# A transformer block on one core: residual sums moved from VectorE to accumulating DMAs, PSUM copies to ScalarE, b2 by DMA, and four more seven-product row pairs

## The chip, the cores and the metric

The kernel runs on one core of a Trainium2 chip. The time is device microseconds of one execution, input and output in HBM, all stages included. Three runs of the kernel before took 364.31, 365.56 and 367.79 us; the median, 365.56, is what the time after is compared with.

## What is computed

One block over 2048 rows of width 576: a layer norm, sliding dilated attention (32 heads of 18, eight keys at distances 0, 2, ..., 14), an output projection with a residual, two layer norms in a row, an MLP of width 4608 with tanh GELU, and a second residual.

```
qkv = (layernorm(x) @ wqkv)                       # 576 -> 3 x 576
logits = q . k[s - 2w] * 18**-0.5, w = 0..7       # masked where s - 2w < 0
o = softmax(logits) . v[s - 2w]
h = x + o @ wo
y = layernorm(layernorm(h))
out = h + (gelu(y @ w1 + b1) @ w2 + b2)           # 576 -> 4608 -> 576
```

## The kernel before

Row s = 16 p + j of the input lies in partition p of tile j, so a tile is 128 rows and there are 16. Keys at even distances are then other tiles of the same parity, with a shift by one partition where the tile number wraps. `kv_ring[r]` holds K and V of the eight tiles of parity r; after tile j has used its own slot, `halo(j, t)` (L336) reloads that slot from `kv_dram` one row shifted, for the tiles that come later in `ATT_ORDER`. In `pv_sum(c)`, `pv_sum(d)` the V halo of tile c must therefore land before the first product of tile d.

The first 68 us compute layer norm and QKV. Then come eight groups of two tiles, `GROUPS`, k = 0 to 7, each of about 36 us. In a group, MLP1 (`mlp1`, 4 visits of two "duos" of PSUM banks) makes the hidden values of the group's two tiles, and MLP2 (`mlp2` in groups 0 and 1, `mlp2_fast` in groups 2 to 7) makes their outputs. Everything else of later tiles is laid into this by hand: the whole schedule is written out, so each engine's queue runs in the order in which the Python emits, with waits on what is not ready. TensorE, ScalarE, VectorE, SP (plain DMAs and DMA transposes) and GpSimd have one queue each. The attention of the tiles two groups on, the projection by wo (`wo_visit`) and layer norm 2 of the next group's tiles c and d lie inside group k.

MLP1 and wo use half-height matmuls in two phases: `phase` 1 of a duo swaps the halves of its banks, and waits for `marker`, a GpSimd no-op which waits for the last matmul of phase 0 (L226). GpSimd's queue thus stands in TensorE's path.

`mlp2_fast` (L682) multiplies row pairs m = 0 to 17 of w2. For the first `rows` of them it uses a scheme of seven products in place of eight, and `plain` does the rest. `ROWS` gives 12, 12, 12, 16, 18 and 18 for groups 2 to 7. The seven products need sums of blocks: `w2_sums` of the weights (once, kept), `h_sums` of the hidden values (each group), both on VectorE. Its list `steps` is the order of work; products are tuples, "b", "d" and "f" are seed copies on ScalarE from one PSUM bank to another (L735), and names like "hc", "h", "6", "7", "in", "exp", "4" are hooks into which the main loop puts work of other tiles. For groups 3 to 6 it begins: wo visit, "hc" (h of tile c and its statistics on ScalarE), product 1, seed "b", "h", product 7, product 2, product 6.

The residual: `x_of(j)` is one of the eight even slots of `x_all`, used by tile j and by its neighbour j + 1 in turn. It holds x until `ln2_h` (L455) forms h = x + wo output. Then it is given h + b2 in one of two ways: `add_b2` on VectorE (groups 0 and 7), or `put_b2`, a DMA of b2 from SBUF, followed by `accumulate_h`, an accumulating DMA of h issued by GpSimd (groups 1 to 6). At the end of MLP2 VectorE adds the PSUM result to it and writes `o_sb`, which SP stores to the output: `finish_out` (L741) in groups 0 and 1; in `mlp2_fast`, `out0` for tile j0 (step "o0"), `do_rest` and `out1` for tile j1 (steps "rest" and "o1"). `reload_x` later loads the x of the other tile into the slot.

Of the kernel before, what the change touches and what calls it, by code (L numbers as in the profile page):

```python
# [17 lines left out]
def kernel(  # L18
# [12 lines left out]
    nc = tc.nc  # L31
# [46 lines left out]
    b2_bc = wpool.tile([P, D], BF16, name="b2_bc")  # L78
# [419 lines left out]
    def add_b2(j):  # L498
        nc.vector.tensor_tensor(out=x_of(j), in0=h_of.pop(j)[:], in1=b2_bc[:], op=ALU.add)

    def put_b2(j):
        nc.sync.dma_start(out=x_of(j), in_=b2_bc[:])

    def accumulate_h(j):
        ins = nc.gpsimd.dma_start(out=x_of(j), in_=h_of.pop(j)[:], accum_op=ALU.add).ins
        tc.add_manual_dep(ins, read[0].name, sync_dep, reason="behind the transposes of LN2")
# [108 lines left out]
    def s_slot(t, m0, m1):  # L615
# [5 lines left out]
        if not ring1_free[0]:  # L621
            return q_all[:, 11 - 2 * i, (m0 - SR) * P:(m1 - SR) * P].bitcast(F16).rearrange("p (m c) -> p m c", c=P)
# [59 lines left out]
    def mlp2_fast(g, rows, tags, wo, hooks, first_wo=False):  # L682
        last = wo is None
# [5 lines left out]
        o0, o1 = (late.tile([P, D], BF16, tag="o_sb", name="o_sb", bufs=2) for _ in range(2))  # L689
        flat = kv_ring[int(rows == NM)][:].rearrange("p w t d -> p (w t d)")  # L690
        rest = q_all[:, 13:16:2, :].bitcast(F32) if SR < rows < NM else halves(flat[:, W * 2 * D - 2 * D:W * 2 * D].bitcast(F32))
# [5 lines left out]
        def out0(n0, n1):  # L697
            add(halves(o0[:])[:, n0:n1], af[:, n0:n1, 0:HALF], halves(x_of(j0))[:, n0:n1])
            nc.sync.dma_start(out=out3[:, j0, n0 * HALF:n1 * HALF], in_=o0[:, n0 * HALF:n1 * HALF])

        def out1():
            add(o1[:, 0:HALF], b, rest[:, 0])
            add(o1[:, HALF:D], bank[5], rest[:, 1])
            nc.sync.dma_start(out=out3[:, j1, :], in_=o1[:])

        def do_rest():
            add(rest, bank[7].unsqueeze(1).to_broadcast([P, 2, HALF]), halves(x_of(j1)))
# [17 lines left out]
        elif not last:  # L725
            steps = ["wo", "hc", (1, all_), "b", "h", "e", (7, lo), (6, all_), "6", "d", "7", (2, all_), (7, hi), "rest", "in",
                     (5, all_), "f", (4, all_), "o1", (3, all_), "o0"]
# [11 lines left out]
    po_of = {}  # L739

    def finish_out(j):  # L741
        o_sb = late.tile([P, D], BF16, tag="o_sb", name="o_sb", bufs=2)
        nc.vector.tensor_tensor(out=o_sb[:].rearrange("p (g c) -> p g c", g=2), in0=po_of.pop(j)[:, :, 0:HALF],
                                in1=halves(x_of(j)), op=ALU.add)
        nc.sync.dma_start(out=out3[:, j, :], in_=o_sb[:])
# [5 lines left out]
    with tc.manual_schedule(engines={ENG.PE, ENG.Activation, ENG.DVE, ENG.SP, ENG.Pool}):  # L751
# [21 lines left out]
        nc.sync.dma_start(out=b2_bc[:], in_=B_b2.partition_broadcast(P))  # L773
# [98 lines left out]
        def ln2_ins(c, d):  # L872
            for j in (c, d):
                ln2_in(j)
            if c not in (GROUPS[2][0], GROUPS[-1][0]):
                accumulate_hs(c, d)
# [13 lines left out]
        for n, v in enumerate((19, 20, 21, 22)):  # L890
# [19 lines left out]
            18: [c_(ln2_rstd, A[0]), c_(add_b2, A[0]), c_(ln2_bias, A[0]), c_(halo, A[2], 1), c_(att_qk_add, A[2], ((0, 0, 9),))],  # L910
            19: [c_(ln2, A[1])],
            20: [c_(ln2_rstd, A[1]), c_(add_b2, A[1]), c_(ln2_bias, A[1]), c_(att_qk_rest, A[2], 0, 1)],
# [63 lines left out]
        ROWS = {2: 12, 3: 12, 4: 12, 5: 16, 6: NM, 7: NM}  # L976
# [3 lines left out]
        for k, g in enumerate(GROUPS):  # L980
# [3 lines left out]
            if k in (1, 2):  # L984
                m1[0].append(c_(finish_out, GROUPS[k - 1][1]))
            if k == 0:
                m1[0] += [c_(halos, 1), c_(load_w2, 4), c_(att_qk_a, d), c_(att_qk_rest, d, 1), c_(halo, d, 1)]
                mid[0] = {1: [c_(exps, d)]}
                m1[1] = [c_(pv_t, c), c_(pv_t, d), c_(att_qk_a, e), c_(halo, e, 1)]
# [4 lines left out]
                ib[0] = [c_(finish_out, g[0]), c_(att_den, e, f), c_(pv_sum, e), c_(send_o, e)]  # L994
                ib[8] = [c_(read_o, e)]
            elif k == 1:
                m1[0] += [c_(pv_sum, d), c_(send_o, d)]
                m1[1] = [c_(att_qk_a, e), c_(halo, e, 1), c_(read_o, d), c_(att_qk_b, e, 0), c_(halos, 7)]
                m1[3] = [c_(att_qk_a, f), c_(halo, f, 1), c_(att_qk_add, f, ((0, 0, 9), (0, 0, 4)))]
# [3 lines left out]
                ib[0] = [c_(finish_out, g[0])]  # L1003
# [88 lines left out]
```

## Time and profile before

| what | value |
|---|---|
| runs | 364.31, 365.56, 367.79 us |
| profiled execution | 364.48 us, span 362.70 |
| TensorE busy, matmuls | 357.4 us (99%), 4891 |
| VectorE busy | 302.0 us (83%) |
| ScalarE busy | 229.5 us (63%) |
| GpSimd busy | 36.7 us (10%) |
| DMA, hardware queue q1 | 41.13 MB, 41.8% of 16 engines |
| DMA, software queue q0 (GpSimd's) | 1.77 MB, 4.7% of 16 engines |
| start of MLP1, groups 0 to 7 | 68.67, 106.73, 144.48, 180.98, 217.25, 253.53, 289.62, 325.67 us |

Busy time is the union of an engine's instructions; those that only issue a DMA or wait are not counted, but the accumulating DMAs on GpSimd are shown with the time that their issue takes. Lines of an engine in order of time give start (us from the start of the span), duration (of all the instructions merged in the line), engine, source line, operation, output and inputs, shapes, count, and in brackets the idle time before it and what ended it. A "border" below is the time at which MLP1 of a group starts.

### The profile page before, as it was taken

What the parts mean: (1) busy time and instruction counts of PE and PEld (TensorE: products, weight loads), DVE (VectorE), ACT (ScalarE), POOL (GpSimd) and SP (SyncE); (2) the same over time, 40 slices, a digit from 0 to 9 for tenths busy, and PEclk for the clock granted to TensorE, in tenths of its full rate; (3) what the DMA queues carried; (4) which work ended last, traced back from release to release, by engine and by line L of the source; (5) the groups of instructions that cost most, each with busy time, mean ns of one, the idle gap of its engine ahead of it and who ended that gap; (6) DMA issues with size and microseconds to landing.
All of it is one profiled execution on the core that took longest, in us unless ns stands there. A gap on an engine that the chain in (4) does not pass through costs nothing.

```text
span 362.7 us, 11409 instructions
## 1 busy us (share of the span) xinstructions
PE 357.4 (99%) x4891; PEld 290.0 (80%) x4891; DVE 302.0 (83%) x422; ACT 229.5 (63%) x507; POOL 36.7 (10%) x47
## 2 busy tenths in 40 slices
PE   8999999999999999999999999999999999999996
PEld 5688777888788877887788778877887788778874
DVE  5899999999999998999899989998899999720431
ACT  4789756798626782668556945694569466706620
POOL 2241004000120020101100210020101100100000
PEclk9999999999999999999999999999999999999999
DMA  8995969973446732621443154514542442120001
GB/s 241 308 264 143 292 175 287 386 254 72 150 88 106 215 122 66 129 63 51 121 88 89 52 126 80 90 51 95 111 78 64 56 93 65 39 54 18 2 2 33
DMA packets 61139, 43.70 MB, mean 120 GB/s; under 512 B 31888, under 2 KB 59408, under 8 KB 61088
## 3 DMA queue, kind: packets, MB, share of 16 engines
q1 hardware_dynamic: 59200, 41.13, 41.8%
q0 software_dynamic: 1728, 1.77, 4.7%
q8 instruction: 38, 0.62, 0.7%
q10 hardware_dynamic: 160, 0.07, 0.1%
q14 instruction: 13, 0.11, 0.1%
HBM read 21.10 MB, written 12.42 MB: 92 GB/s over the span
## 4 chain that ended last, share of the span: by engine, by line
PE 93%; DMA 3%; ACT 1%; DVE 1%; issue 0%; SPq 0%; ACTq 0%
PE pm L217 38%; PE po L664 25%; PE pq L217 14%; PE po L576 10%; PE pw L217 5%; DMA oT<-td 2%; ACT h_all L557 1%; DMA xnT<-xd 1%; PE xt_pt L182 1%; DMA x_all<-in_A_x_dram 1%; DVE kv_ring L644 0%; PE xt_pt L186 0%; ACT q_all L816 0%; PE h_pt L182 0%; PE o_pt L182 0%
## 5 line engine op out<-in xcount | busy, mean ns | idle before, releaser
L557 ACT ACTIVATE h_all<-pm,b_sb 128x256 f16<-128x256 f32 (+1 forms) x288 | 108.7, 496 | 70.2 <-PE pm L217 69.6
L217 PE MATMUL pm<-hnT,w_sb 64*128 64x256 bf16 x2304 | 143.0, 269 | 0.0
L217 PEld LDWEIGHTS <-w_sb 64*128 64x128 bf16 x2304 | 111.7, 94 | 15.1 <-issue 1.7
L664 PEld LDWEIGHTS <-h_all 128*128 128x128 f16 x512 | 49.4, 98 | 14.4 <-issue 1.6
L217 PE MATMUL pq<-wq_sb,xnT 64*128 64x288 bf16 x768 | 54.4, 283 | 0.4 <-DMA xnT<-xd 0.4
L217 PEld LDWEIGHTS <-xnT 64*128 64x128 bf16 x864 | 41.4, 94 | 11.6 <-DMA xnT<-xd 0.7
L348 DVE TENSOR_TENSOR prod<-prod 128x2304 bf16<-128x2304 bf16 (+1 forms) x64 | 44.2, 691 | 2.0
L394 DVE TENSOR_TENSOR prod<-kv_ring,probs 128x4608 bf16<-128x4608 bf16 x16 | 40.9, 2555 | 2.5 <-DMA kv_ring<-kv_dram 2.1
L342 DVE TENSOR_TENSOR prod<-kv_ring,q_all 128x4608 bf16<-128x4608 bf16 x16 | 40.8, 2548 | 0.2
L217 PE MATMUL pm<-hnT,w1h_sb 64*128 64x256 bf16 x288 | 39.2, 269 | 0.0
L664 PE MATMUL po<-w2a_sb,h_all 128*128 128x288 bf16 (+1 forms) x282 | 38.9, 286 | 0.0
L400 DVE TENSOR_TENSOR prod<-prod 128x2304 bf16<-128x2304 bf16 (+1 forms) x32 | 33.9, 1058 | 1.1
L576 PEld LDWEIGHTS <-h_all 128*128 128x128 bf16 x288 | 27.9, 98 | 7.9 <-issue 1.0
L664 PEld LDWEIGHTS <-kv_ring 128*128 128x128 f16 x252 | 24.6, 98 | 6.3
L478 POOL TENSOR_TENSOR ln_rstd<-ln_var,mhalf 128x1 f32<-128x1 f32 x13 | 11.7, 899 | 169.7 <-ACT ln_var L477 169.7
L576 PE MATMUL po<-w2a_sb,h_all 128*128 128x288 bf16 x224 | 28.5, 286 | 0.0
L664 PE MATMUL po<-w2b_sb,h_all 128*128 128x288 bf16 (+1 forms) x142 | 21.5, 286 | 0.2 <-DVE h_all L644 0.2
L217 PE MATMUL pw<-wo_sb,oT 64*128 64x288 bf16 x256 | 19.6, 283 | 0.4 <-DMA oT<-td 0.3
L644 DVE TENSOR_TENSOR kv_ring<-h_all 128x1536 f16<-128x1536 f16 (+3 forms) x9 | 6.8, 753 | 15.3 <-ACT h_all L557 15.3
L735 ACT COPY po<-po 128x288 f32<-128x288 f32 x18 | 6.9, 384 | 19.3 <-PE po L664 19.3
L162 POOL TENSOR_TENSOR ln_rstd<-ln_veps,mhalf 128x1 f32<-128x1 f32 (+2 forms) x14 | 13.4, 967 | 48.5 <-DVE ln_veps L156 33.2
L217 PEld LDWEIGHTS <-oT 64*128 64x128 bf16 x288 | 13.6, 94 | 4.9 <-DMA oT<-td 1.1
(110 smaller groups left out, 387.5 us busy)
## 6 DMA issues: line engine op xcount, KB each, us to landing
w_sb<-in_B_w_dram SPq DMA_DIRECT2D x6, 768.0 KB, 6.8
kv_ring<-kv_dram SPq DMA_DIRECT2D x28, 144.0 KB, 2.8
w2a_sb<-in_B_w_dram SPq DMA_DIRECT2D x4, 1008.0 KB, 7.4
kv_dram<-kv_ring SPq DMA_DIRECT2D x13, 288.0 KB, 3.0
out_dram<-o_sb SPq DMA_DIRECT2D x15, 144.0 KB, 2.7
td<-q_all SPq DMA_DIRECT2D x14, 144.0 KB, 1.9
td<-hn SPq DMA_DIRECT2D x14, 144.0 KB, 1.8
x_all<-in_A_x_dram SPq DMA_DIRECT2D x12, 144.0 KB, 2.8
```

What stands on the lines that cost most here:

```text
L162: nc.gpsimd.tensor_tensor(out=rstd[:], in0=veps[:], in1=mhalf[:].to_broadcast([P, n]), op=ALU.pow)
L217: last = nc.tensor.matmul(duo["g"][r ^ swap][i], lhsT=lhsT, rhs=rhs, start=(swap == 0 and i == 0 and kt == 0), stop=(swap == 1 and kt == K ...
L342: nc.vector.tensor_tensor(out=prod[:], in0=k_ring[j % 2], in1=q_all[:, j, :].unsqueeze(1) .to_broadcast([P, W, D]), op=ALU.mult)
L348: nc.vector.tensor_tensor(out=prod[:, :, o * H:o * H + n], in0=prod[:, :, a * H:a * H + n], in1=prod[:, :, c * H:c * H + n], op=ALU.add)
L394: nc.vector.tensor_tensor(out=prod[:].rearrange("p w (d h) -> p w d h", h=H), in0=v_ring[j % 2].rearrange("p w (d h) -> p w d h", h=H), in ...
L400: nc.vector.tensor_tensor(out=prod[:, 0:n, :], in0=prod[:, 0:n, :], in1=prod[:, n:2 * n, :], op=ALU.add)
L478: nc.gpsimd.tensor_tensor(out=rstd[:], in0=var[:], in1=mhalf[:], op=ALU.pow)
L557: pace[0] = nc.scalar.activation(out=hT(grp)[:, f, 0:N], in_=ps[:, r, i * N:(i + 1) * N], func=ACT.Gelu_apprx_tanh, bias=b1_sb[:, f:f + 1] ...
L576: nc.tensor.matmul(banks[half], lhsT=hT(grp)[:, f, i * P:(i + 1) * P], rhs=w2_rows(f)[:, half * HALF:(half + 1) * HALF], start=(f == 0), s ...
L644: nc.vector.tensor_tensor(out=s_slot(t, m0, m1), in0=a, in1=b, op=alu)
L664: nc.tensor.matmul(bank, lhsT=l, rhs=r, start=start, stop=stop, skip_group_check=True)
L735: nc.scalar.copy(out=bank[seed[step][1]], in_=bank[seed[step][0]])
```

## The change

- In groups 0 to 5 the output is summed in `x_of(j)`: ScalarE copies the PSUM result to a float32 `o_sb`, GpSimd adds it to `x_of(j)` by an accumulating DMA (`out_sum`), and SP stores `x_of(j)` (`out_store`). For tile j1 in groups 2 to 5, ScalarE copies the common part ("rest"), and VectorE's two half adds join it to the two banks. Groups 6 and 7 keep the adds of before.
- `b2_bc` is gone; `put_b2` reads b2 from HBM, broadcast over the partitions, for all sixteen tiles, and `add_b2` is gone.
- The accumulates of h move: out of `ln2_ins` (hook "in") into hook "4", behind step "o1"; those of groups 0 and 1 into visits 1 and 2 of their own MLP1.
- Group 4 has 16 seven-product row pairs in place of 12; the w2 sums of pairs 12 to 15 that are still missing are made in group 4 (before `h_sums` ahead of MLP1's last visit) in place of group 5.

```diff
-    def add_b2(j):
-        nc.vector.tensor_tensor(out=x_of(j), in0=h_of.pop(j)[:], in1=b2_bc[:], op=ALU.add)
-
     def put_b2(j):
-        nc.sync.dma_start(out=x_of(j), in_=b2_bc[:])
+        nc.sync.dma_start(out=x_of(j), in_=B_b2.partition_broadcast(P))
...
         def out0(n0, n1):
-            add(halves(o0[:])[:, n0:n1], af[:, n0:n1, 0:HALF], halves(x_of(j0))[:, n0:n1])
+            if summed:
+                nc.scalar.copy(out=halves(o0), in_=af[:, :, 0:HALF])
+                return
+            add(halves(o0)[:, n0:n1], af[:, n0:n1, 0:HALF], halves(x_of(j0))[:, n0:n1])
...
         def out1():
+            if summed:
+                add(o1[:, HALF:D], bank[5], o1[:, 0:HALF])
+                add(o1[:, 0:HALF], b, o1[:, 0:HALF])
+                out_sum(j1)
+                return
...
         def do_rest():
+            if summed:
+                nc.scalar.copy(out=o1[:, 0:HALF], in_=bank[7])
+                return
...
+    def out_sum(j):
+        nc.gpsimd.dma_start(out=x_of(j), in_=o_of.pop(j), accum_op=ALU.add)
+
+    def out_store(j):
+        nc.sync.dma_start(out=out3[:, j, :], in_=x_of(j))
 
     def finish_out(j):
-        o_sb = late.tile([P, D], BF16, tag="o_sb", name="o_sb", bufs=2)
-        nc.vector.tensor_tensor(out=o_sb[:].rearrange("p (g c) -> p g c", g=2), in0=po_of.pop(j)[:, :, 0:HALF],
-                                in1=halves(x_of(j)), op=ALU.add)
-        nc.sync.dma_start(out=out3[:, j, :], in_=o_sb[:])
+        nc.scalar.copy(out=halves(new_o(j, True)), in_=po_of.pop(j)[:, :, 0:HALF])
...
         def ln2_ins(c, d):
             for j in (c, d):
                 ln2_in(j)
-            if c not in (GROUPS[2][0], GROUPS[-1][0]):
-                accumulate_hs(c, d)
...
-        ROWS = {2: 12, 3: 12, 4: 12, 5: 16, 6: NM, 7: NM}
+        ROWS = {2: 12, 3: 12, 4: 16, 5: 16, 6: NM, 7: NM}
...
             if k in (1, 2):
                 m1[0].append(c_(finish_out, GROUPS[k - 1][1]))
+                m1[1], m1[3] = [c_(accumulate_hs, *g)], [c_(out_store, GROUPS[k - 1][1])]
+                m1[2] = [c_(out_sum, GROUPS[k - 1][1])]
+            elif 2 < k < 7:
+                m1[0].append(c_(out_store, GROUPS[k - 1][1]))
+                m1[1], m1[3] = [c_(out_sum, GROUPS[k - 1][0])], [c_(out_store, GROUPS[k - 1][0])]
+            if k == 2:
+                m1[0].append(c_(out_store, GROUPS[1][0]))
...
-                ib[0] = [c_(finish_out, g[0]), c_(att_den, e, f), c_(pv_sum, e), c_(send_o, e)]
-                ib[8] = [c_(read_o, e)]
+                ib[0] = [c_(finish_out, g[0]), c_(out_sum, g[0]), c_(att_den, e, f), c_(pv_sum, e), c_(send_o, e)]
+                ib[8] = [c_(read_o, e), c_(out_store, g[0])]
...
+                if k == 4:
+                    m1[3] += [c_(w2_sums, 12, 14, (2, 3)), c_(w2_sums, 14, 16, (2, 3))]
                 m1[3] += [c_(h_sums, 0, min(rows, SR), early)]
...
                 x["in"] = [c_(ln2_ins, c, d)] + x["in"]
+                x["4"] = [c_(accumulate_hs, c, d)] + x["4"]
```

`m1[v]` is emitted before visit v of MLP1; `ib[f]` before row f of the second tile's MLP2.

## The prediction

> **What bounds the kernel now.** I read the page first, then stages, then each engine in order of time around the borders between groups.
>
> From the page: busy shares, granted clock and chain of waits.
>
> ```profile
> PE 357.4 (99%) x4891; PEld 290.0 (80%) x4891; DVE 302.0 (83%) x422; ACT 229.5 (63%) x507; POOL 36.7 (10%) x47
> ...
> PEclk9999999999999999999999999999999999999999
> ...
> PE 93%; DMA 3%; ACT 1%; DVE 1%; issue 0%; SPq 0%; ACTq 0%
> ```
>
> TensorE is the bound and the clock is full. Busy times by stage show whether it is also packed; the rows are groups 3, 4, 5 and 6 (start of MLP1 to the next group's start).
>
> ```profile
> 180.98:217.25 36.27, 36.27 (x495) 30.26 (x496) 33.20 (x37) 23.96 (x57) 4.99 (x6) 1.00 0.39 88
> 217.25:253.53 36.28, 36.28 (x495) 30.28 (x496) 33.31 (x37) 23.95 (x57) 2.82 (x3) 1.00 0.40 77
> 253.53:289.62 36.09, 35.99 (x490) 29.71 (x492) 33.35 (x42) 22.93 (x56) 3.80 (x6) 1.00 0.43 80
> 289.62:325.67 36.05, 35.71 (x489) 29.60 (x490) 26.22 (x38) 19.70 (x49) 2.17 (x4) 1.00 0.28 63
> ```
>
> The first two numbers after the window are its length and TensorE's busy time: groups 3 and 4 have no gap. Two remain, in the wo visits of groups 5 and 6, where TensorE waits for the transposed attention output oT. TensorE in order of time:
>
> ```profile
> 271.65 0.29 PE L217 MATMUL pw<-woh_sb,oT 64*128 64x288 bf16 x2
> 272.03 0.66 PE L217 MATMUL pw<-wo_sb,oT 64*128 64x288 bf16 x8
> ...
> 307.74 0.29 PE L217 MATMUL pw<-woh_sb,oT 64*128 64x288 bf16 x2
> 308.37 0.66 PE L217 MATMUL pw<-wo_sb,oT 64*128 64x288 bf16 x8 [0.34 <-DMA oT<-td]
> ```
>
> Elsewhere the next piece starts 0.12 us after the two-matmul piece; here 0.38 and 0.63, so 0.26 and 0.51 us are lost. So little can be won; what decides is how close to late the engines that feed TensorE are. VectorE has 33 of 36 us, and group 4 shows the margin. VectorE, ScalarE and TensorE in order of time:
>
> ```profile
> 234.60 0.88 DVE L644 TENSOR_TENSOR kv_ring<-h_all 128x1536 f16<-128x1536 f16 x1
> 235.52 0.96 DVE L644 TENSOR_TENSOR h_all<-h_all 128x1536 f16<-128x1536 f16 x1
> 236.80 1.42 DVE L458 TENSOR_TENSOR h<-pw,x_all 128x576 f32<-128x576 f32 x2 [0.33 <-PE pw L217]
> ...
> 237.64 0.77 ACT L475 ACTIVATE hn<-h 128x576 bf16<-128x576 f32 x1
> ...
> 239.63 0.39 ACT L735 COPY po<-po 128x288 f32<-128x288 f32 x1
> ...
> 237.18 4.58 PE L664 MATMUL po<-w2a_sb,h_all 128*128 128x288 bf16 x36
> ```
>
> VectorE makes h with only 0.33 us to spare; ScalarE takes the statistics of h and then the seed copy of step "b", which ends at 240.02. TensorE's product 2 adds into the bank which that copy reads, and comes 24 matmuls after 237.18: 24 x 0.1235 = 2.96, at 240.14 (0.1235 is group 3's 16.28 us of MLP2 over 132). A later h delays TensorE almost one for one.
>
> **The change part by part.** All sums are against the profiled execution: 364.48 us, of which 362.70 is span. The median of the runs is 1.08 above it, added at the end.
>
> *Products.* Group 4 goes from 12 to 16 seven-product pairs: four matmuls fewer, -4 x 0.1235 = -0.49 us on TensorE.
>
> *VectorE.* Removed: four finish_out adds and four add_b2 (0.749 each), four o0 and four rest adds of groups 2 to 5 (0.756): 12.0 us. Added: group 4's h_sums for pairs 12 to 15, 1.49 (group 5's four ran from 277.45 to 278.94). Moved: two w2_sums calls, 1.47 (278.94 to 280.41), from group 5's MLP2 to ahead of group 4's h. Most of the relief is not on TensorE's path; where it falls matters. Losing o0, VectorE starts pv_sum of the next group 0.9 us earlier in groups 3 and 4 (180.79 against 181.69; 217.07 against 217.97), since the old add waited for the last matmul.
>
> *ScalarE.* Eight 128x576 copies (0.65, the nearest row is L312 from PSUM) and four of 128x288 (0.384): 6.7 us. They hide: between the last exp table work and the first gelu of the next group ScalarE idles 5.56 us (251.17 to 256.73), and the copy of "rest" falls where it waits 1.0 for TensorE. Queued behind them are gelus; without that cover each would cost its duration. I take 0.
>
> *GpSimd.* Accumulating DMAs go from 12 to 28 (16 for h, 12 for outputs). This is what the issues, the landings and the queue show now:
>
> ```profile
> L505 POOL DMA_DIRECT2D x_all<-h x12: 886/1122/1236, 106.0 to 289.4; - x12
> DMA to landing us min/median/max: 3.1/3.9/5.5
> ...
> q0 software_dynamic: 1728, 1.77, 4.7%
> ```
>
> Behind them on GpSimd's queue stand the markers that let TensorE swap halves of a bank; the first one after a border is needed 2.2 us after MLP1 starts (two first phases of 20 matmuls, 0.055 each). At the last border into group 5 the two accumulates ended at 255.41, MLP1 having begun at 253.53: 1.88 after it. Three in a row could end 2.4 after it. Bounds 0 and 1.2 us (one more issue) at a border; at the borders into groups 3 and 4 they end 1.05 and 0.32 after it, so I take 0. The Trainium skill (SBUF, State Buffer, the section with the "DVE blocks DMA" trap) warns that a VectorE instruction in a two-port mode keeps GpSimd from writing descriptors, and elsewhere on the page that tensor_tensor has no such mode. By the warning alone each issue could wait for one 2.56 us add and three would break the margin; the rows above, 886 to 1236 ns beside a VectorE 92% busy, show no such wait.
>
> *DMA engines.* The q0 share is 0.047 x 362.7 / 12 = 1.42 us of all sixteen engines for one accumulate; sixteen more are 23 us, off the path except where somebody waits. Somebody does: in pv_sum, tile d's first product needs the halo that SP fetches after tile c's. VectorE, SP and GpSimd around the border into group 5:
>
> ```profile
> 261.16 2.56 DVE L394 TENSOR_TENSOR prod<-kv_ring,probs 128x4608 bf16<-128x4608 bf16 x1 [1.70 <-DMA kv_ring<-kv_dram]
> ...
> 256.82 0.33 SPq L339 DMA_DIRECT2D kv_ring<-kv_dram  x1
> ...
> 253.63 1.78 POOL L505 DMA_DIRECT2D x_all<-h  x2 [9.66 <-DMA x_all<-in_A_x_dram]
> ```
>
> The halo came 1.41 us after the accumulates' end and landed 4.3 us after issue, against a median of 2.8; after a gap of 2.24 (group 3) nobody waited. In the change VectorE is 0.9 earlier in groups 3 and 4, so the gap falls to about 1.35, and the output sum of j0 is issued just then (behind the second marker, 2.2 after MLP1's start). So tile d starts between 0.9 earlier (halo unhindered) and 1.6 later (halo 5.2 us after issue) than now; I take 0.7 later, as the gap matches group 5's. The Trainium skill (DMA: Bandwidth & Descriptors, Anatomy of one DMA) gives 2.0 us plus bytes over 436 GB/s for a GpSimd DMA, an estimate of 2.3 us for 147 KB. By it the accumulates would be gone when the halo comes and the sum below would be -0.9; the rows say 3.9, so the sum goes by the rows.
>
> *What that does to TensorE.*
> - Group 3: h is late by 0.7 - 0.40 (idle before it now) = 0.3, less 0.12 margin: 0.2 (0 to 1.1).
> - Group 4: 0.7 + 1.47 - 0.33 = 1.84 late; sixteen pairs put product 2 at 28 matmuls, 3.45, and the seed now ends 2.84 after MLP2's start, so 0.61 is free: 1.2 (0 to 2.1).
> - Start of group 5's MLP1: hnT follows the late h, and no gap exists now: 0.3 (0 to 1.0).
> - Group 5's oT: tile d again behind the accumulates, while MLP1 starts 0.49 earlier: 0.5 (0 to 1.1) in place of 0.26.
> - Group 6: VectorE was last there (the old rest waited for nothing at 288.40) and loses 1.47 + 0.756 ahead of it: the 0.51 gap goes (or stays).
>
> *SP.* Twelve output stores now read x_all and wait for an accumulate. At a border the first stands ahead of the halo: issued about 2.4 before MLP1's start, plus 3.9, it is released at +1.5, and SP needs to be free at +2.4. Cover 0.9 us; beyond it the halo is late, inside the 1.6 above. The second is issued after the visits' oT reads and waits for nothing. Sixteen put_b2 read HBM instead of twelve reading SBUF: 2.0 us now, 2.8 for x from HBM, needed ten us later: 0. Dropping the early load of b2 (behind all loads of x): 0.
>
> *Groups 0 to 2.* finish_out moves to ScalarE behind its exps (104.29 in group 0, where GpSimd's accumulates stood at 105.96 anyway); its results are read by nobody for 4 us or more; accumulates moved into MLP1 come one visit later, with 3.9 us between the last marker of a visit and the first need of the next. 0; bounds 0 and 0.5.
>
> Sum: -0.49 + 0.2 + 1.2 + 0.3 + (0.5 - 0.26) - 0.51 = +0.94: 365.4 profiled, 366.5 as a median. Lower ends: -0.49 - 0.26 - 0.51 = -1.26: 364.3. Upper ends: -0.49 + 1.1 + 2.1 + 1.0 + 0.84 + 0 + 0.5 = +5.0: 370.6.
>
> **The rivals.**
> *Clean gain.* Halos pass the accumulates and nothing is late: 364.3. For it: no gap at all in groups 2 to 4 now, and 10.5 us less work on VectorE. Against it: margins of 0.12 to 0.61 us and the 1.70 us wait already seen. It needs tile d's start no later than now.
> *Accumulates swamp the borders: slower.* The DMA share is 0.82 to 0.85 in the four us around a border already, with two accumulates; four stand there afterwards. If the halo has both output sums in front of it, tile d is one more accumulate (1.42) beyond the upper end in groups 3, 4 and 5: 370.6 + 4.3 = 374.9. It decides from a halo landing 0.9 us later than I take it at these three borders: +2.7 us, 369.2. Between that and the far end I price it at 371, near the upper ends.
> *The relief is worth more than 1%.* TensorE would have to lose 3.66 us of work or gaps; only 1.26 are in sight.
>
> **How the numbers follow.** About 1% (3.66 us) is what a measurement of this kernel tells from no change. The forecast, a small loss within 1%, gets 0.42; the clean gain 0.20; swamped borders 0.34; faster by over 1% 0.04. So faster 0.04, same 0.62, slower 0.34. Time 366.5; the range, 363.9 (clean gain, less what runs differ) to 371, leaves out the far end of the swamped case.
>
> **What would show it.** TensorE waits on ScalarE's seed copy in group 4's MLP2 (after 28 matmuls), on oT in group 5, and no longer in group 6; VectorE waits for kv_ring in pv_sum of groups 3 to 5. It is wrong if VectorE shows no such waits, if TensorE waits on GpSimd's markers, or if SP stands at an output store while a halo is due.

## The result and the profile after

| what | before | after |
|---|---|---|
| median of 18 runs of each (lowest to highest) | 365.57 us (364.31 to 370.23) | 369.55 us (367.46 to 371.81) |
| time after / before, 95% interval | | 1.010 (1.0073 to 1.0127) |
| profiled execution, its span | 364.48, 362.70 us | 368.69, 366.88 us |

The kernel became slower by 4.0 us, 1.0%: on the border between "no change" and "slower by over 1%". The forecast was 366.5, the range 363.9 to 371.0.

First the page of the changed kernel: busy shares, clock, the software DMA queue, the chain of waits.

```profile
PE 357.8 (98%) x4887; PEld 292.2 (80%) x4887; DVE 293.0 (80%) x410; ACT 235.6 (64%) x519; POOL 49.8 (14%) x63
...
PEclk9999999999999999999999999999999999999999
...
q0 software_dynamic: 4032, 4.13, 10.2%
...
PE 69%; DVE 14%; DMA 9%; issue 3%; ACT 2%; SPq 2%; POOL 1%; DVEq 0%; POOLq 0%; ACTq 0%
```

TensorE has its four matmuls less, the clock is as full as before, and VectorE lost 9 us (the prediction had 10.5). All of that is as intended. But the share of TensorE in the chain of waits fell from 93% to 69%, while VectorE's rose from 1 to 14 and that of DMA from 3 to 9: there are now times at which TensorE waits for VectorE, and VectorE for a DMA. GpSimd's queue takes 10.2% of the DMA engines in place of 4.7.

Busy times by stage say where. The rows are groups 0, 3, 4, 5 and 6 of the kernel after; the columns are the window, its length, and busy time of TensorE matmul, TensorE weight load, VectorE, ScalarE and GpSimd, then clock, DMA share and GB/s.

```profile
69.09:109.27 40.18, 38.41 (x509) 31.17 (x504) 35.23 (x46) 29.60 (x64) 4.25 (x5) 1.00 0.60 178
...
183.52:219.79 36.27, 36.27 (x494) 30.27 (x494) 31.75 (x36) 24.82 (x59) 5.03 (x8) 1.00 0.47 96
219.79:258.38 38.59, 36.33 (x489) 29.86 (x489) 34.79 (x44) 25.44 (x60) 6.09 (x6) 1.00 0.43 83
258.38:294.17 35.79, 35.79 (x489) 29.80 (x490) 32.78 (x39) 24.40 (x59) 4.94 (x7) 1.00 0.48 91
294.17:329.90 35.73, 35.71 (x488) 29.61 (x488) 22.66 (x32) 19.27 (x48) 3.71 (x5) 1.00 0.40 79
```

And group 0 of the kernel before, which the prediction did not show:

```profile
68.50:106.67 38.17, 38.17 (x509) 31.29 (x504) 36.69 (x47) 28.55 (x62) 2.14 (x3) 1.00 0.56 171
```

Here group 0 is counted from the first matmul of MLP1; the 68.67 and 106.73 of the table of before are where the chain of waits enters the groups, a little later. Two groups lost time: group 0 (40.18 against 38.17, +2.01) and group 4 (38.59 against 36.28, +2.31). Group 3 is as long as before, groups 5 and 6 are 0.30 and 0.32 shorter. Start-up, ahead of group 0, is 0.59 longer, which is no more than executions differ by: in the six profiled kernels with the start-up of before, group 0 begins between 68.50 and 70.33. Groups 1, 2 and 7 are 0.11 shorter together. The sum is +4.18, the difference of the spans.

**Group 4.** All engines in order of time, kernel after; "DVE L457" makes h, "ACT L743" are the seed copies "b" (243.85) and "d" (249.90), "ACT L174" at 249.13 is layer norm's second pass over tile d, "POOL L477" its reciprocal root.

```profile
239.30 0.94 DVE L641 TENSOR_TENSOR kv_ring<-h_all 128x1536 f16<-128x1536 f16 x1
239.78 1.89 PE L661 MATMUL po<-w2a_sb,h_all 128*128 128x288 bf16 x14
240.28 0.96 DVE L641 TENSOR_TENSOR h_all<-h_all 128x1536 f16<-128x1536 f16 x1
241.15 1.42 DVE L457 TENSOR_TENSOR h<-pw,x_all 128x576 f32<-128x576 f32 x2
241.94 0.69 ACT L474 ACTIVATE hn<-h 128x576 bf16<-128x576 f32 x1 [1.50 <-DVE h L457]
...
243.85 0.39 ACT L743 COPY po<-po 128x288 f32<-128x288 f32 x1
244.10 0.75 POOL L477 TENSOR_TENSOR ln_rstd<-ln_var,mhalf 128x1 f32<-128x1 f32 x1 [20.41 <-ACT ln_var L476]
...
244.29 1.88 PE L661 MATMUL po<-w2a_sb,h_all 128*128 128x288 bf16 x14 [0.70 <-ACT po L743]
...
245.81 2.55 DVE L341 TENSOR_TENSOR prod<-kv_ring,q_all 128x4608 bf16<-128x4608 bf16 x1
...
246.32 2.45 POOL L477 TENSOR_TENSOR ln_rstd<-ln_var,mhalf 128x1 f32<-128x1 f32 x1 [1.47 <-ACT ln_var L476]
...
248.80 0.30 ACT L482 ACTIVATE ln_nmean<-ln_nmean,ln_rstd 128x1 f32<-128x1 f32 x1 [1.54 <-POOL ln_rstd L477]
...
249.13 0.87 ACT L174 ACTIVATE hn<-h,ln_nmean,ln_rstd 128x576 bf16<-128x576 f32 x1
249.90 0.39 ACT L743 COPY po<-po 128x288 f32<-128x288 f32 x1
...
250.34 1.63 PE L661 MATMUL po<-x_all,kv_ring 128*128 128x288 f16 x12 [0.99 <-ACT po L743]
...
258.38 0.61 PE L216 MATMUL pm<-hnT,w_sb 64*128 64x256 bf16 x8 [0.53 <-DMA hnT<-td]
```

MLP2 starts at 239.78 and h is made 1.37 us behind it; before it was made 0.38 ahead of MLP2 (236.80 against 237.18). From there everything is late in a row: the seed copy "b" (TensorE waits, first matmul 0.87 late), GpSimd's second reciprocal root, which takes 2.45 us where the first took 0.75, the pass over tile d behind it, the seed copy "d" behind that on ScalarE's queue (TensorE 1.15 late), and hnT of the next group (0.69 late). Product 7 starts another 0.20 late: its first matmul, at 241.96, follows the first half of h, which ends at 241.91 and reads the bank that product 7 takes (in two later runs the profile names h for the wait at this place). So TensorE starts its matmuls 2.9 us late in all; four fewer matmuls (0.49) leave about the 2.3 by which the group grew.

Why the second reciprocal root takes so long can be read from the kernel before, where the same pair of instructions stands in group 4; there nothing waited for it:

```profile
241.01 2.55 DVE L342 TENSOR_TENSOR prod<-kv_ring,q_all 128x4608 bf16<-128x4608 bf16 x1
...
242.10 1.87 POOL L478 TENSOR_TENSOR ln_rstd<-ln_var,mhalf 128x1 f32<-128x1 f32 x1 [1.59 <-ACT ln_var L477]
```

In both kernels it begins while VectorE's 2.55 us product runs, and ends 0.41 us after that product has ended (243.97 after 243.56; 248.77 after 248.36).

**Group 0.** All engines in order of time, kernel after; L338 is the reload of a halo, L501 an accumulate of h, L393 VectorE's product in `pv_sum`, L192 the write of tile c's attention output to `td` in HBM, and L198 its transpose back as oT.

```profile
72.13 1.05 POOL L501 DMA_DIRECT2D x_all<-h  x1 [9.48 <-PE pm L216]
...
75.97 0.88 POOL L501 DMA_DIRECT2D x_all<-h  x1 [2.78 <-PE pm L216]
...
79.73 0.34 SPq L192 DMA_DIRECT2D td<-q_all  x1
...
83.90 2.56 DVE L393 TENSOR_TENSOR prod<-kv_ring,probs 128x4608 bf16<-128x4608 bf16 x1 [2.85 <-DMA kv_ring<-kv_dram]
...
84.47 1.22 SPq L198 DMA_TRANSPOSE oT<-td  x1
...
87.41 0.66 PE L216 MATMUL pw<-wo_sb,oT 64*128 64x288 bf16 x8 [1.34 <-DMA oT<-td]
```

And the kernel before:

```profile
81.10 2.56 DVE L394 TENSOR_TENSOR prod<-kv_ring,probs 128x4608 bf16<-128x4608 bf16 x1
...
81.75 2.31 SPq L199 DMA_TRANSPOSE oT<-td  x1
```

The halo is issued at 77.05 and `td` written from 79.73 in both kernels. Before, tile d's product started at 81.10 and waited for nothing, and the transpose was issued at 81.75. Now two DMAs land late. VectorE waits 2.85 us for the halo; and SP waits 3.8 us (before: 1.1) until `td` has landed, so that the transpose is issued at 84.47 and TensorE stands 1.48 us at the wo visit. That visit needs oT of tile c, and not tile d's product: the halo is not what it waits for. By the chain of waits the late halo is felt at the other gap of group 0, 0.60 at the border into group 1, where hnT is late. The DMA share by windows of 2 us, 78 to 82, shows why both are late; the kernel before, then after:

```profile
78.00:80.00 2.00, 2.00 (x42) 1.78 (x38) 1.93 (x4) 2.00 (x7) 0.00 (x0) 1.00 0.36 99
80.00:82.00 2.00, 2.00 (x42) 1.79 (x38) 1.90 (x4) 2.00 (x7) 0.00 (x0) 1.00 0.28 82
```

```profile
78.00:80.00 2.00, 2.00 (x40) 1.78 (x38) 1.93 (x4) 1.99 (x7) 0.00 (x0) 1.00 1.06 364
80.00:82.00 2.00, 2.00 (x42) 1.78 (x38) 0.98 (x3) 2.00 (x7) 0.00 (x0) 1.00 1.12 235
```

The two columns at the end are the DMA share and the GB/s. The engines are full with weight loads until 78 in both kernels; before, they were free when the halo came, now they work until 82. The two accumulates take 1.23 us each of all sixteen engines by their packets, and the last weight load (`w2b_sb`) lands 12.0 us after its issue in place of 9.6. Over all profiled kernels that load takes 11.9 to 12.4 us in the four that have the accumulates here and 8.7 to 10.4 in the ten that do not. Besides, it is issued 2.02 us after the start of the group in place of 0.95.

**The borders.** VectorE's waits, the group for halos in `pv_sum` (in total, times, longest), after:

```profile
DVE prod L393 <- DMA kv_ring<-kv_dram: 6.2, 5, 2.8
```

Before it was 2.1 us in two waits, the longest 1.7. The waits are where they were forecast, 0.58, 1.04 and 0.66 us in groups 3, 4 and 5; the longest, 2.85, is that of group 0. In this execution TensorE lost nothing by them in groups 3 and 5.

### The profile page after: what moved, and what is told of

It reads as the page before. It is cut to its first block, busy times and chain, and to the rows that moved or that the text cites. A ratio compares the mean times of both kernels' runs of the same rounds, so it can differ in the third digit from the quotient of the medians.

```text
span 366.9 us, 11432 instructions
## 1 busy us (share of the span) xinstructions
PE 357.8 (98%) x4887; PEld 292.2 (80%) x4887; DVE 293.0 (80%) x410; ACT 235.6 (64%) x519; POOL 49.8 (14%) x63
## 3 DMA queue, kind: packets, MB, share of 16 engines
q0 software_dynamic: 4032, 4.13, 10.2%
## 4 chain that ended last, share of the span: by engine, by line
PE 69%; DVE 14%; DMA 9%; issue 3%; ACT 2%; SPq 2%; POOL 1%; DVEq 0%; POOLq 0%; ACTq 0%
PE pm L216 29%; PE po L661 20%; PE pq L216 11%; PE po L573 5%; PE pw L216 4%; DVE prod L347 3%; DMA kv_ring<-kv_dram 3%; DVE prod L393 3%; DVE prod L341 2%; DMA hnT<-td 2%; DMA td<-hn 1%; DMA xnT<-xd 1%; DMA wq_sb<-in_A_wqkv_dram 1%; DVE prod L399 1%; ACT h_all L554 1%
## 5 line engine op out<-in xcount | busy, mean ns | idle before, releaser
L216 PEld LDWEIGHTS <-w_sb 64*128 64x128 bf16 x2304 | 113.6, 94 | 14.4 <-issue 1.9
L661 PEld LDWEIGHTS <-h_all 128*128 128x128 f16 x496 | 47.8, 98 | 15.1 <-issue 2.7
L393 DVE TENSOR_TENSOR prod<-kv_ring,probs 128x4608 bf16<-128x4608 bf16 x16 | 40.9, 2558 | 6.6 <-DMA kv_ring<-kv_dram 6.2
L341 DVE TENSOR_TENSOR prod<-kv_ring,q_all 128x4608 bf16<-128x4608 bf16 x16 | 40.8, 2549 | 0.2
L661 PE MATMUL po<-w2a_sb,h_all 128*128 128x288 bf16 (+1 forms) x272 | 37.5, 286 | 0.7 <-ACT po L743 0.7
L477 POOL TENSOR_TENSOR ln_rstd<-ln_var,mhalf 128x1 f32<-128x1 f32 x13 | 11.5, 882 | 137.8 <-ACT ln_var L476 137.8
L661 PE MATMUL po<-w2b_sb,h_all 128*128 128x288 bf16 (+1 forms) x132 | 20.6, 286 | 0.1
L501 POOL DMA_DIRECT2D x_all<-h x16 | 15.1, 1142 | 36.9 <-PE pm L216 20.4
L743 ACT COPY po<-po 128x288 f32<-128x288 f32 x18 | 6.9, 385 | 18.6 <-PE po L661 18.5
```

The lines of the kernel that those rows point to most:

```text
L216: last = nc.tensor.matmul(duo["g"][r ^ swap][i], lhsT=lhsT, rhs=rhs, start=(swap == 0 and i == 0 and kt == 0), stop=(swap == 1 and kt == K ...
L341: nc.vector.tensor_tensor(out=prod[:], in0=k_ring[j % 2], in1=q_all[:, j, :].unsqueeze(1) .to_broadcast([P, W, D]), op=ALU.mult)
L393: nc.vector.tensor_tensor(out=prod[:].rearrange("p w (d h) -> p w d h", h=H), in0=v_ring[j % 2].rearrange("p w (d h) -> p w d h", h=H), in ...
L477: nc.gpsimd.tensor_tensor(out=rstd[:], in0=var[:], in1=mhalf[:], op=ALU.pow)
L661: nc.tensor.matmul(bank, lhsT=l, rhs=r, start=start, stop=stop, skip_group_check=True)
L743: nc.scalar.copy(out=bank[seed[step][1]], in_=bank[seed[step][0]])
```

## The experiments

The questions were: how much of the 1.0% lies in group 0, how much in group 4, how much at the borders; whether it is the order of the work that loses the time, which can be mended, or the accumulating DMAs as such (the rival). Twelve kernels, in three lots; each lot has its own runs of the kernel before, and ratios are to those, with 95% intervals. An interval is about 0.26% to each side, so the difference of two ratios is known to about 0.37%; differences below that are given as estimates.

**Group 4 with 12 row pairs, as before**, and the weight sums again in group 5; all else as after.

```diff
-        ROWS = {2: 12, 3: 12, 4: 16, 5: 16, 6: NM, 7: NM}
+        ROWS = {2: 12, 3: 12, 4: 12, 5: 16, 6: NM, 7: NM}
...
-                if k == 4:
-                    m1[3] += [c_(w2_sums, 12, 14, (2, 3)), c_(w2_sums, 14, 16, (2, 3))]
...
-                    x["h"] += [c_(h_sums, SR, rows)]
+                    x["h"] += [c_(h_sums, SR, rows), c_(w2_sums, 12, 14, (2, 3)), c_(w2_sums, 14, 16, (2, 3))]
```

> The changed kernel with group 4 back at 12 seven-product pairs and the two w2_sums calls back in group 5's MLP2. Theory A (the loss sits in two places: group 4, where h and the seeds come late, about 2.9 us of gaps; group 0, where DMAs are late, about 2.1 us): group 4's gaps go, four matmuls (0.49 us) come back, so 2.2 to 2.6 us faster than the changed kernel, about 367.2, ratio to before 1.004; the gaps before group 0's wo visit and at the border into group 1 (together about 2.1 us) stay. Theory B (accumulates swamp every border): the loss stays near 1.010, less at most 0.3%.

Measured: 1.0074 (1.0048 to 1.0100), median 367.55. Group 4 is 36.89 us long with one gap of 0.62 at seed "b"; group 0 stands 1.70 us at its wo visit as before this edit. So the estimate for the 16 pairs is 1.010 - 1.0074 = 0.26%, net of the 0.49 us that they save; by the times alone it is not clear of noise, but the profile shows the gaps gone.

**Group 0 with VectorE's add of b2**, as before; all else as after.

```diff
+    def add_b2(j):
+        nc.vector.tensor_tensor(out=x_of(j), in0=h_of.pop(j)[:], in1=b2_bc[:], op=ALU.add)
...
-            20: [c_(ln2_rstd, A[1]), c_(put_b2, A[1]), c_(ln2_bias, A[1]), c_(att_qk_rest, A[2], 0, 1)],
+            20: [c_(ln2_rstd, A[1]), c_(add_b2, A[1]), c_(ln2_bias, A[1]), c_(att_qk_rest, A[2], 0, 1)],
...
-                m1[1] = [c_(pv_t, c), c_(pv_t, d), c_(att_qk_a, e), c_(halo, e, 1), c_(accumulate_h, g[0])]
-                m1[2] = [c_(accumulate_h, g[1])]
+                m1[1] = [c_(pv_t, c), c_(pv_t, d), c_(att_qk_a, e), c_(halo, e, 1)]
```

> The changed kernel with group 0's residual prepared as before (b2 kept in SBUF, add_b2 on VectorE, no put_b2 and no accumulates of h in group 0). Theory A: the gaps in group 0 (1.48 us before the wo visit, 0.60 us at the border) go, group 4's 2.9 us stay: 2 us faster than the changed kernel, about 367.5, ratio 1.0045. Theory B: ratio stays at 1.009 or above. Theory C (b2 read from HBM and put on SP is the cost in group 0, not the accumulates) gives the same here; it is told apart by a later run that moves only the accumulates.

Measured: 1.0065 (1.0039 to 1.0091), median 367.33. Group 0 has no gap above 0.15 us and is 38.16 long; tile d's product there waits for nothing. So the estimate for group 0's two b2 loads and two accumulates together is 0.35%, about 1.3 us; again the profile is clearer than the times.

**The kernel before with 16 pairs in group 4**, the sums ahead of h as in the change.

```diff
-        ROWS = {2: 12, 3: 12, 4: 12, 5: 16, 6: NM, 7: NM}
+        ROWS = {2: 12, 3: 12, 4: 16, 5: 16, 6: NM, 7: NM}
...
+                if k == 4:
+                    m1[3] += [c_(w2_sums, 12, 14, (2, 3)), c_(w2_sums, 14, 16, (2, 3))]
...
-                if k == 5:
-                    x["h"] += [c_(h_sums, SR, rows), c_(w2_sums, 12, 14, (2, 3)), c_(w2_sums, 14, 16, (2, 3))]
+                if rows > SR:
+                    x["h"] += [c_(h_sums, SR, rows)]
```

> The kernel before with one part of the change alone: 16 seven-product pairs in group 4, w2_sums in group 4 ahead of h. Residual sums as before. Theory A: h is late in group 4 by 1.47 less 0.33 us (no o0 relief), the seed d stands behind the sends of hn: gaps of 1 to 3 us in group 4, less 0.49 us, net +0.5 to +2.4 us, ratio 1.0015 to 1.0065. Theory B: no accumulates are added, so no gaps: -0.49 us, ratio 0.9985.

Measured: 1.0029 (1.0006 to 1.0052), median 365.61. TensorE stands 0.37 and 1.16 us in group 4, at the seeds. So the sums ahead of h lose time without any of the other edits.

**The change with group 4's weight sums moved behind h** (hook "h", behind `h_sums`).

```diff
-                if k == 4:
-                    m1[3] += [c_(w2_sums, 12, 14, (2, 3)), c_(w2_sums, 14, 16, (2, 3))]
...
+                if k == 4:
+                    x["h"] += [c_(w2_sums, 12, 14, (2, 3)), c_(w2_sums, 14, 16, (2, 3))]
```

> The changed kernel with the two w2_sums calls of group 4 moved from ahead of h (before h_sums in MLP1) to hook h of group 4's MLP2, behind its h_sums; same work, later. Theory A: h comes 1.5 us earlier, the gap at product 2 (0.87 and 0.20 us) goes or shrinks to under 0.3, hnT is about 1.4 us earlier so the gap at the border into group 5 (0.69) goes; the seed d stays behind the send of tile d: 1.2 to 2.3 us faster than the changed kernel, 367.2 to 368.4, ratio 1.004 to 1.0075. Theory B: within 0.5 us of the changed kernel.

Measured: 1.0058 (1.0031 to 1.0086), median 367.43: better than the change by an estimated 0.42%. Groups 4 and 5 of this kernel by stage:

```profile
218.24:254.16 35.92, 35.92 (x489) 29.88 (x489) 33.36 (x42) 24.17 (x58) 3.65 (x6) 1.00 0.45 89
254.16:291.77 37.61, 36.13 (x490) 29.72 (x490) 34.06 (x41) 25.77 (x61) 5.88 (x8) 1.00 0.43 87
```

Group 4 has no gap left and is 2.67 us shorter than in the change. Its engines in order of time:

```profile
238.68 1.42 DVE L457 TENSOR_TENSOR h<-pw,x_all 128x576 f32<-128x576 f32 x2
239.47 0.69 ACT L474 ACTIVATE hn<-h 128x576 bf16<-128x576 f32 x1 [0.58 <-DVE h L457]
241.38 0.39 ACT L743 COPY po<-po 128x288 f32<-128x288 f32 x1
...
243.85 0.72 POOL L477 TENSOR_TENSOR ln_rstd<-ln_var,mhalf 128x1 f32<-128x1 f32 x1 [1.47 <-ACT ln_var L476]
...
244.81 2.55 DVE L341 TENSOR_TENSOR prod<-kv_ring,q_all 128x4608 bf16<-128x4608 bf16 x1
...
245.94 0.38 ACT L743 COPY po<-po 128x288 f32<-128x288 f32 x1
```

GpSimd's second reciprocal root takes 0.72 us here and not 2.45: it is over before VectorE begins the 2.55 us product of L341, because the weight sums now stand between. What was won is partly lost again in this execution: group 5 is 37.61, with 1.16 at its oT and 0.64 at a product that waits for `h_sums`.

**The change with group 0's two accumulates of h moved from visits 1 and 2 to visit 3.**

```diff
-                m1[1] = [c_(pv_t, c), c_(pv_t, d), c_(att_qk_a, e), c_(halo, e, 1), c_(accumulate_h, g[0])]
-                m1[2] = [c_(accumulate_h, g[1])]
+                m1[1] = [c_(pv_t, c), c_(pv_t, d), c_(att_qk_a, e), c_(halo, e, 1)]
+                m1[3] = [c_(accumulate_hs, *g)]
```

> The changed kernel with the two accumulates of h in group 0 both moved from ahead of visits 1 and 2 to ahead of visit 3 of group 0's MLP1, about 8 us later, when the w2 loads have ended; b2 still comes from HBM through SP. Theory A (the accumulates hold up the w2 load, the halo and tile c's transposes): the gap before group 0's wo visit falls from 1.5-1.7 to under 0.7 us, ratio 1.005 to 1.008. Theory C (put_b2 and SP's later w2 loads are the cost): the gap stays above 1.2 us and the ratio near 1.010.

Measured: 1.0084 (1.0058 to 1.0109), median 368.80 of 6 runs. All engines in order of time, group 0 of this kernel:

```profile
80.96 1.97 POOL L501 DMA_DIRECT2D x_all<-h  x2 [17.42 <-DMA w2b_sb<-in_B_w_dram]
...
82.72 2.56 DVE L393 TENSOR_TENSOR prod<-kv_ring,probs 128x4608 bf16<-128x4608 bf16 x1 [0.75 <-DMA kv_ring<-kv_dram]
...
83.32 1.46 SPq L198 DMA_TRANSPOSE oT<-td  x1
...
87.75 0.66 PE L216 MATMUL pw<-wo_sb,oT 64*128 64x288 bf16 x8 [0.71 <-DMA oT<-td]
```

The wait for the halo falls to 0.75 us; in the four kernels that leave the accumulates where the change put them it is 2.15, 2.55, 2.85 and 3.34. The last weight load lands 9.8 us after its issue, as without the accumulates. So the accumulates hold up that load and the halo: that is shown. But the gap at the wo visit, 0.85 here, was 0.81, 0.84, 1.48 and 1.70 in those four, and the time is within the noise of the change. The trace shows where this gap comes from: the transpose of oT is issued 13.26 us after the start of the group, as in the kernel before (13.25; 15.38 in the change), but it now lands 4.4 us after its issue in place of 2.9. The two accumulates, issued from 80.96, stand beside it; that they slow it is likely and was not tested. Moving them is no cure. What the two b2 loads cost in group 0 stays open.

**Both undone: group 4 with 12 pairs and group 0 with the add** (the first two edits together).

```diff
-        ROWS = {2: 12, 3: 12, 4: 16, 5: 16, 6: NM, 7: NM}
+        ROWS = {2: 12, 3: 12, 4: 12, 5: 16, 6: NM, 7: NM}
...
-                m1[2] = [c_(accumulate_h, g[1])]
```

> The changed kernel with both undone: group 4 at 12 pairs with the sums back in group 5, and group 0's residual prepared as before. What is left of the change is the residual by accumulating DMAs in groups 0 to 5 and b2 by DMA from group 1 on. Theory A: the two losses were all there is, and oT is no longer late: ratio 0.9985 to 1.0015. Theory B (four accumulates at a border make oT and h late at borders by turns): gaps of 0.5 to 1.5 us at one or two of the wo visits or seeds of groups 3 to 6 stay, ratio 1.003 to 1.006.

Measured: 1.0041 (1.0016 to 1.0066), median 366.61. Neither of the two places is left: together they are worth an estimated 0.59%, and 0.41% is still there. The estimates of the parts agree: group 0 is worth 1.010 - 1.0065 = 0.35% or, from the other side, 1.0074 - 1.0041 = 0.33%; group 4 is worth 0.26% or 1.0065 - 1.0041 = 0.24%; with the 0.41% that makes 1.0%. Each single part is smaller than its uncertainty of about 0.37%; the two together and the rest are not.

**The change with j0's output sums one visit later** (groups 3 to 6), to clear the border of one accumulate.

```diff
-                m1[1], m1[3] = [c_(out_sum, GROUPS[k - 1][0])], [c_(out_store, GROUPS[k - 1][0])]
+                m1[2], m1[3] = [c_(out_sum, GROUPS[k - 1][0])], [c_(out_store, GROUPS[k - 1][0])]
...
```

> The changed kernel with the output sum of tile j0 in groups 3 to 6 moved from ahead of visit 1 to ahead of visit 2 of MLP1, 4.4 us later, out of the way of the halo of tile c; same work. Theory B: VectorE's waits for kv_ring in pv_sum of groups 3 to 5 (0.58, 1.04, 0.66 us) go under 0.4 each and the ratio falls by 0.001 to 0.004. Theory A: group 4's h gets earlier by at most 0.5 us, the rest stays: ratio 1.008 to 1.010.

Measured: 1.0086 (1.0057 to 1.0115), median 368.97 of 6 runs. By the time this is inconclusive: an effect of the expected size drowns in the interval. The profile says more: VectorE's waits for the halos of groups 3, 4 and 5 did not fall but are 0.85, 1.05 and 1.24 us against 0.58, 1.04 and 0.66 (in all 5.5 against 6.2, because groups 0 and 1 wait less). In group 4 the sum is now issued at 224.66, behind the halo of 220.74 and no longer beside it. So j0's output sum is not what those halos wait behind.

**The kernel before with one more accumulate per pair.** Between the two accumulates of h stands a third, of h of tile d into a spare tile that nobody reads: six more in all, and nothing else changed.

```diff
+        junk = []
...
-            for j in js:
-                accumulate_h(j)
+            accumulate_h(js[0])
+            nc.gpsimd.dma_start(out=junk[0][:], in_=h_of[js[1]][:], accum_op=ALU.add)
+            accumulate_h(js[1])
...
+        junk.append(late.tile([P, D], BF16, name="junk"))
+        nc.gpsimd.memset(junk[0][:], 0.0)
```

> The kernel before with one more accumulating DMA of the same size at each place where two stand (h of tile d into a spare tile that nobody reads; the output is unchanged): three in place of two, six more in all. Theory B: halo and oT are late at the borders, gaps at wo visits of groups 3 to 6 grow by 0.5 to 1.5 us in all, ratio 1.002 to 1.005. Theory A: no more than 0.3 us, ratio under 1.001.

Measured: 1.0071 (1.0047 to 1.0096), median 367.39 (365.49 to 370.19): more than was expected, 2.2 to 2.6 us for six DMAs that nobody waits for. The software queue on this kernel's page and VectorE's waits for halos:

```profile
q0 software_dynamic: 2592, 2.66, 6.9%
```

```profile
DVE prod L394 <- DMA kv_ring<-kv_dram: 5.1, 5, 1.7
```

The queue's share rose from 4.7% to 6.9%: 2.2% of 363.7 us over six is 1.33 us of all sixteen engines for each accumulate, and the waits for halos rose from 2.1 to 5.1 us. So one more accumulate at a border costs time although nobody reads its result. No gap of TensorE stands at a GpSimd marker here, so the longer stretch of issues on GpSimd's queue is not the reason. The profiled execution was the fastest of its eleven, 1.9 below the median, so it shows the smallest share of that cost: gaps of 0.41 and 0.45 at oT and 0.28 and 0.27 at a seed.

**The same with a plain copy** in place of the additional accumulate (`accum_op` left out), issued by GpSimd at the same place, same bytes.

> The kernel before with one more DMA at each place where two accumulates stand, as in the run with an extra accumulate (ratio 1.0071), but a plain copy of h of tile d to the spare tile, issued by GpSimd, same bytes read and written, without the addition. If the sixteen DMA engines' time for the addition is the cost (153 to 171 ns a packet against 52 for plain ones): ratio 1.000 to 1.003. If one more DMA on GpSimd's queue or one more DMA at that place is the cost, whatever it does: 1.005 to 1.008.

Measured: 1.0026 (1.0002 to 1.0050), median 366.31.

```profile
q0 software_dynamic: 2592, 2.66, 6.1%
```

Same packets and bytes, 6.1% in place of 6.9: 0.85 us of all engines for a copy (0.91 to 1.00 by the copies' own packets; those of the additional accumulates take 1.29 to 1.46). The cost is lower, but the two intervals overlap a little, and the copy is not free. That accumulating is worse than copying is likely, not settled. VectorE's waits for halos are 6.5 us here, more than with the additional accumulate (5.1): the total of these waits in one execution does not tell the cost in time.

**The kernel before with b2 read from HBM** in groups 1 to 6.

```diff
-        nc.sync.dma_start(out=x_of(j), in_=b2_bc[:])
+        nc.sync.dma_start(out=x_of(j), in_=B_b2.partition_broadcast(P))
```

> The kernel before with one part of the change alone: put_b2 of groups 1 to 6 reads b2 from HBM, broadcast, in place of SBUF (add_b2 in groups 0 and 7 stays). If the source of b2 has a share in the 0.41% that is left with both other parts undone: ratio above 1.002 (packets of 84 ns against 51, landing 3.8 us against 2.0). If the accumulates alone make it: 0.999 to 1.0015.

Measured: 1.0004 (0.9980 to 1.0028). No cost is seen; group 0, where the change has two such loads, is not in this test.

**The kernel before with 16 pairs, sums behind h, and seed "d" ahead of hook "7"** in groups 4 and 5: the only part of the change that promised a gain, put where it should not hurt.

```diff
-                else ["wo", "hc", (1, all_), "b", "h", "e", (7, lo), (2, all_), (6, all_), "6", "7", "d", "11", (7, hi), "rest"]
+                else ["wo", "hc", (1, all_), "b", "h", "e", (7, lo), (2, all_), (6, all_), "6", "d", "7", "11", (7, hi), "rest"]
...
+                if k == 4:
+                    x["h"] += [c_(w2_sums, 12, 14, (2, 3)), c_(w2_sums, 14, 16, (2, 3))]
```

> The kernel before with 16 pairs in group 4, but with the w2_sums behind h (hook h of group 4) and the seed d ahead of the send of tile d (hook 7) in groups 4 and 5. No accumulates are added. If lateness of h and of the seed d is the whole cost of the 16 pairs: four matmuls fewer, -0.49 us, ratio 0.998 to 0.9995. If VectorE's 1.49 us more of h_sums make o1 and the attention of group 5 late instead: 1.000 to 1.004.

Measured: 0.9983 (0.9960 to 1.0005), median 364.53 against 364.93. That is the size of the saving of four matmuls (0.49 of 365 us is 0.13%), with an interval that reaches no change.

**The change with all of it mended**: sums behind h, seed "d" ahead of "7", group 0 as before, j0's output sums one visit later; each line as in the experiment that it comes from.

```diff
-                m1[2] = [c_(accumulate_h, g[1])]
...
-                if k == 4:
-                    m1[3] += [c_(w2_sums, 12, 14, (2, 3)), c_(w2_sums, 14, 16, (2, 3))]
...
+                if k == 4:
+                    x["h"] += [c_(w2_sums, 12, 14, (2, 3)), c_(w2_sums, 14, 16, (2, 3))]
```

> The changed kernel with what the runs point to put together: 16 pairs with the sums behind h and the seed d ahead of hook 7, group 0's residual prepared as before, output sums of j0 ahead of visit 2. The accumulating DMAs of groups 0 to 5 stay. If the accumulates at the borders keep their price (1.0041 with rows 12): ratio 1.002 to 1.004. If the relief on VectorE pays once nothing else is late: below 1.000.

Measured: 1.0014 (0.9994 to 1.0034), median 365.38 (364.70 to 366.62). About 0.9 of the 1.0% is recovered and the spread of the runs shrinks from 4.4 to 1.9 us, but the kernel before is not beaten. No version here is clearly faster than the kernel before.

## Why the prediction was right or wrong

The time lies inside the range, but in the region of the "swamped borders" rival (from 369.2 on), not of the forecast: +0.94 in the profiled execution was forecast, +4.18 came. Of the 3.24 between them, 3.16 is two terms that the sum did not have: 1.15 us at seed "d" in group 4, and 2.01 in group 0, which the sum put at 0. The delays that it did name in group 4 and at the next border came, 0.87 for 1.2 and 0.69 for 0.3. That the time is still inside the range is in part luck: the upper end was made of delays in groups 3 and 5 that did not come in this execution. Step by step:

- **Products, -0.49.** Held: 4887 matmuls, and the mended version of this part alone measures 0.9983 (0.9960 to 1.0005).
- **Group 4, +1.2 and +0.3 at the next border.** Right in its mechanism, mis-sized: h was forecast 1.84 us late and came 1.75 late (from 0.38 ahead of MLP2 to 1.37 behind it); product 2 stood 0.87 (forecast 1.2), the border 0.69 (forecast 0.3). The term that was missing is 1.15 us at seed "d". With 16 pairs group 4 takes another order of steps, in which "d" is emitted behind hook "7", so on ScalarE behind the pass over tile d, which waits for GpSimd. And GpSimd's reciprocal root was held up by VectorE. In the traces of before and after each of these instructions in a group's MLP2 that begins while the 128x4608 product of L341 (two inputs in SBUF) runs ends 0.40 to 0.42 us after that product: 248.36 and 248.77 above; in the kernel before 207.29 and 207.69, 243.56 and 243.97. It took 2.45 us in group 4 in all five kernels profiled that do the sums ahead of h with 16 pairs, and 0.72, 0.61 and 0.72 in the three that do them behind h, where the product begins later. The Trainium skill (SBUF — State Buffer, Who interferes with whom) has this rule: a VectorE instruction with two SBUF inputs contends with a GpSimd instruction that reads SBUF, and the port pair that they share is an exclusive lock. The traces agree with it. The prediction looked at the trap for DMAs on the same page and not at this rule, which bears on seed "d". A product did not hold up the issue of a DMA: the accumulate issued at 75.97, in the middle of VectorE's 2.56 us product of 74.47, took 0.88 us.
- **Groups 0 to 2, "0; bounds 0 and 0.5".** This is the step that failed. It asked who reads the results of the moved accumulates, and nobody does for 4 us; it did not ask what else is on the DMA engines at 72 to 78 us. They are full there with weight loads, and with two accumulates they are full until 82, over a halo and over tile c's `td`, which TensorE's wo visit needs. Profile: +2.01; by the runs an estimated 0.33 to 0.35%, 1.2 to 1.3 us, for accumulates and b2 loads together.
- **Borders, +0.2 in group 3 and +0.24 in group 5.** Tile d starts 0.2 and 0.7 later against the border in groups 3 and 4, where 0.7 was taken. In group 5 it starts 1.4 earlier (6.26 us after the border in place of 7.70), and TensorE's wait for oT there, forecast to grow to 0.5, is gone: that sign did not come. The profiled execution shows no loss on TensorE in groups 3 and 5, even a gain of 0.30 in group 5. The prediction had the halo behind j0's output sum; moving that sum away left the waits as long, so what the halo waits behind is not shown. Yet with both other places undone 0.41%, 1.5 us, remain in the median, and six accumulates more cost the kernel before 0.71%. A single profile is one draw: gaps of up to 1.4 us appear at an oT in group 3, 5 or 6, in one execution here and in the next there. What stays open is the cause of the 0.41%, which holds all remaining parts of the change (copies on ScalarE, stores that read `x_all`, the later accumulates of h): that the accumulates are its cause is made likely by the experiment with additional ones, not isolated.
- **Group 6, -0.51.** Held in the main: the gap is 0.19 in place of 0.51, the group 0.32 shorter.
- **Zeros.** The copies on ScalarE, GpSimd's markers, the output stores on SP: no gap of TensorE stands at any of them. b2 from HBM lands in 3.8 us in place of 2.0, and in groups 1 to 6 no cost is seen (1.0004, 0.9980 to 1.0028).
- **The price of an accumulate.** The sum went by the row of 3.9 us to landing; with 28 in place of 12 the median for h became 4.8 (3.3 to 7.0). The estimate of 2.3 from the page of the Trainium skill (DMA: Bandwidth & Descriptors, Anatomy of one DMA) is far from both, and the measurement decides.

Of the rivals, "clean gain" is dead: tile d did start later in groups 3 and 4, and the time rose. "Swamped borders", priced at 371 and given 0.34, has the time but not its sign: the profiled execution does not show halos 0.9 us later than taken at three borders. What speaks for it is the 0.41% that is left without groups 0 and 4, and the cost of six more accumulates at the borders; the other 0.6% are the two places that the experiments took out.

## What to carry to other kernels

Work that is moved off a busy engine onto DMA is not free because nobody reads its result soon: look at the DMA share in the few microseconds where it lands, and at which load on somebody's path lies in them. Before adding work ahead of the first instruction of a chain (here h), follow the chain through every queue to its end, in the order that the new version will really use, including whom a long instruction on a neighbouring engine keeps out. And where contention decides, judge by many runs: one profile shows where time can go, not how much goes on average.

## What the hardware showed that was not expected

- A one-column instruction on GpSimd (L477, L478 in the kernel before) takes 0.55 us at its shortest and 2.45 when VectorE's 2.55 us product of two SBUF tensors has just begun; it ends 0.40 to 0.42 us after that product.
- An accumulating DMA of 144 KB takes 1.33 us of all sixteen DMA engines, a plain copy of the same bytes by the same queue 0.85 (both from the shares of the software queue).
- Six accumulates that nobody waits for cost 0.71% (0.47 to 0.96) of a kernel whose DMA engines are, by its page, less than half busy (41.8% and 4.7%).
